# Chunk stages at fixed distances with feed-forward units spread evenly between them, in an RWKV-6 attention kernel with a leaky-ReLU feed-forward

## The chip, the cores and the metric

The kernel runs on one core of a Trainium2 chip. The metric is the device time of one execution in microseconds, the median of several runs. Beside the timed runs there is one profiled execution, whose span (from its first to its last instruction) and own time are given below.

A core has five engines that run side by side, each through its own instructions in a fixed order: PE (TensorE, matmuls and transposes; its weight loads are listed as PEld), DVE (VectorE), ACT (ScalarE), POOL (GpSimd) and SP (SyncE), which here only issues transfers. Matmul results land in PSUM, which has 8 banks of 128 x 512 f32.

## The reference

Attention with a decaying state: 4 batches, 8 heads, 768 steps, head size 48. The result goes through a feed-forward part with a leaky ReLU: 3072 tokens of 384 features, 2048 hidden features, 384 outputs.

```python
for t in range(S):
    cur = np.einsum('bhd,bhe->bhde', u[None] * kt, vt)
    y[:, :, t] = np.einsum('bhd,bhde->bhe', rt, state + cur)
    state = wt[:, :, :, None] * state + np.einsum('bhd,bhe->bhde', kt, vt)
x = y.transpose(0, 2, 1, 3).reshape(B * S, H * D)
h = x @ w_in
out = np.maximum(0.01 * h, h) @ w_out
```

## The kernel before

The tokens are cut into 24 chunks of 128, six to each batch. Within a chunk the recurrence is written as matrix products; between the chunks of a batch a state of 48 x 48 per head is carried on. A chunk goes through five stages, each a function that issues instructions on several engines:

- `s_decay` (lines 124 to 165) issues the chunk's four loads on SP, takes the logarithm of w (ACT, L131), sums it over the steps by two matmuls and four small ones into `cum` (PE, L133 to L140), takes the exponential (ACT, L141), and makes `rd`, `kd` and `el`, the decayed r and k and the decay of the whole chunk (DVE, L144, L145, L148). GpSimd makes `vb` (L151), the products r*u and r*u*k (`t1`, `t2`, L154, L156) and, after a sum on DVE (L160), `vsc` (L162), the part of a step that comes from its own k and v.
- `s_trans` (L167) transposes `rd` and `kd` on PE into `trp` (L172), and DVE copies it to `rkT` (L176).
- `s_scores` (L179) multiplies them into two banks `at` (L186), and DVE masks these into `mt` (L192).
- `s_mix` (L197) makes `y` on PE from the carried state (L206) and the scores (L212); DVE adds `vsc` and gives `ysb` (L218). Then it makes `kv` (L225), DVE adds the old state (`tt`, L232), and GpSimd multiplies by `el` into the next state `st` in two steps (L237). The next chunk's L206 needs that state.
- `s_out` (L244) transposes `ysb` on PE into `ytr` (L248), and ACT copies it into `xT` (L249), which holds all tokens, features across partitions.

The feed-forward part works on blocks of 256 tokens, two chunks. One unit of `m_hidden` (L257) fills a PSUM bank `hp` with two groups of 128 hidden features by 6 matmuls of 256 columns (L264), and ACT writes the leaky ReLU of it to `gt` (L268). One unit of `m_out` (L270) does 8 matmuls of 384 columns (L276) into `op`, half the sum over the hidden features for 128 tokens; after the second half ACT copies it to `osb` (L282) and SP sends it out (L284). A block is 8 hidden units and 4 output units.

PSUM: `cum` has two banks, `trp` and `ytr` share one, the tag `att` (`at` twice, `y`, `kv`) has three, and the tag `mlp` (`hp` and `op`) has two.

PE's order is the order in which the functions are called, under `manual_schedule`. The order on the other engines is made by the framework. The calls come from a small planner (L295 to L337) with costs and latencies of its own: a stage that is due goes first, and feed-forward units otherwise, as soon as their block's tokens are there; at most three chunks are under way. In the order that comes out, the twelve units of a block always stand together, and between two blocks stand some ten stages of two to four chunks. From the third block on, with a stage written by its first letter (D decay, T transposes, S scores, M mix, O out) and h and o for the units:

```
h2*8 o2*4 T7 M6 T8 S7 O6 D9 S8 M7 M8 T9 O7 D10 O8 D11 h3*8 o3*4 S9 T10 T11 S10 M9 S11 M10 O9 D12 M11 h4*8 o4*4
```

It begins with `D0 T0 S0 D1 M0 T1 O0 S1 D2 M1 T2 O1 h0*8 o0*4` and ends with `h10*8 o10*4 O22 O23 h11*8 o11*4`.

Of the kernel before, what the change touches and what calls it, by code (L numbers as in the profile page):

```python
# [8 lines left out]
F32 = mybir.dt.float32  # L9
BF16 = mybir.dt.bfloat16  # L10
AF = mybir.ActivationFunctionType
# [5 lines left out]
def kernel(  # L17
# [11 lines left out]
    nc = tc.nc  # L29
    B, H, S, D = r.shape  # L30
    L = 128
    assert S % L == 0 and H == 8 and D == 48
    C = S // L
    NCH = B * C
    NP = H // 2
    DM = H * D
    KT = DM // 128
    FF = moe_w_in.shape[1]
    NFT = FF // 128
    NOUT = moe_w_out.shape[1]  # L40
    MB = 256
    NBLK = B * S // MB
    CPB = MB // L
    assert DM % 128 == 0 and FF % 256 == 0 and (B * S) % MB == 0 and NOUT <= 512

    const = ctx.enter_context(tc.tile_pool(name="const", bufs=1))
    inpool = ctx.enter_context(tc.tile_pool(name="inpool", bufs=6))
    work = ctx.enter_context(tc.tile_pool(name="work", bufs=3))
    gpool = ctx.enter_context(tc.tile_pool(name="gpool", bufs=2))
    ps_cum = ctx.enter_context(tc.tile_pool(name="ps_cum", bufs=1, space=bass.MemoryType.PSUM))  # L50
    ps_tr = ctx.enter_context(tc.tile_pool(name="ps_tr", bufs=1, space=bass.MemoryType.PSUM))
    ps_att = ctx.enter_context(tc.tile_pool(name="ps_att", bufs=3, space=bass.MemoryType.PSUM))
    ps_mlp = ctx.enter_context(tc.tile_pool(name="ps_mlp", bufs=2, space=bass.MemoryType.PSUM))
# [5 lines left out]
        out=tri[:], in_=tri[:], compare_op=ALU.is_gt, fill=0.0, base=0,  # L59
# [5 lines left out]
        out=trin[:], in_=trin[:], compare_op=ALU.is_ge, fill=0.0, base=0,  # L65
# [20 lines left out]
    w_in_b = const.tile([128, KT, FF], BF16, name="w_in_b")  # L86
    w_out_b = const.tile([128, NFT, NOUT], BF16, name="w_out_b")
    xT = const.tile([128, KT, B * S], BF16, name="xT")
# [20 lines left out]
    for q in range(4):  # L109
        nc.gpsimd.dma_start(  # L110
            out=w_in_b[:, :, q * FQ : (q + 1) * FQ],
            in_=moe_w_in[:, q * FQ : (q + 1) * FQ].rearrange("(t p) n -> p t n", p=128),
        )
    for q in range(2):
        hf = NFT // 2
        nc.gpsimd.dma_start(
            out=w_out_b[:, q * hf : (q + 1) * hf, :],
            in_=moe_w_out[q * hf * 128 : (q + 1) * hf * 128, :].rearrange("(t p) n -> p t n", p=128),
# [3 lines left out]
    att = {}  # L122
# [120 lines left out]

    def s_out(i):  # L244
        a = att.pop(i)
        ytr = ps_tr.tile([128, KT, 128], BF16, name="ytr", tag="tr")
        for t in range(KT):
            nc.tensor.transpose(ytr[:, t, :], a["ysb"][:, t * 128 : (t + 1) * 128], ident[:])  # L248
        nc.scalar.copy(out=xT[:, :, i * L : (i + 1) * L], in_=ytr[:])  # L249

    stages = (s_decay, s_trans, s_scores, s_mix, s_out)


    gts = {}
    ops = {}

    def m_hidden(q, j2):  # L257
        if j2 == 0:
            gts[q] = gpool.tile([128, NFT, MB], BF16, name="gt")
        hp = ps_mlp.tile([128, 2, MB], F32, name="hp", tag="mlp")  # L260
        for jj in range(2):
            j = 2 * j2 + jj
            for t in range(KT):
                nc.tensor.matmul(  # L264
                    hp[:, jj, :], lhsT=w_in_b[:, t, j * 128 : (j + 1) * 128],
                    rhs=xT[:, t, q * MB : (q + 1) * MB], start=(t == 0), stop=(t == KT - 1),
                )
        nc.scalar.activation(out=gts[q][:, 2 * j2 : 2 * j2 + 2, :], in_=hp[:], func=AF.Prelu, alpha=0.01)  # L268

    def m_out(q, ts, hf):  # L270
        if hf == 0:
            ops[q, ts] = ps_mlp.tile([128, NOUT], F32, name="op", tag="mlp")
        op = ops[q, ts]
        half = NFT // 2
        for j in range(hf * half, (hf + 1) * half):
            nc.tensor.matmul(  # L276
                op[:], lhsT=gts[q][:, j, ts * 128 : (ts + 1) * 128], rhs=w_out_b[:, j, :],
                start=(j == 0), stop=(j == NFT - 1),
            )
        if hf == 1:  # L280
            osb = work.tile([128, NOUT], F32, name="osb")
            nc.scalar.copy(out=osb[:], in_=op[:])  # L282
            row = q * MB + ts * 128
            nc.sync.dma_start(out=out[row : row + 128, :], in_=osb[:])  # L284

    mlp = []
    for q in range(NBLK):
        for j2 in range(NFT // 2):
            mlp.append((q, 0.66, m_hidden, (q, j2)))
        for ts in range(CPB):  # L290
            for hf in range(2):
                mlp.append((q, 1.3, m_out, (q, ts, hf)))


    cost = (0.55, 0.6, 0.6, 1.0, 0.25)  # L295
    lat = (2.6, 1.2, 1.9, 1.2, 0.9)
    ready = {}
    for i in range(NCH):
        ready[i, 0] = 6.0 + 6.0 * i
    done_out = {}  # L300
    now = 0.0
    nxt = [0] * NCH
    head = 0
    m = 0
    AHEAD = 3
    with tc.manual_schedule(engines={mybir.EngineType.PE}):
        while head < NCH or m < len(mlp):
            cands = []
            for i in range(head, min(head + AHEAD, NCH)):
                s = nxt[i]  # L310
                if s < 5 and (s, i) and (i == 0 or nxt[i - 1] > s):
                    cands.append((ready[i, s], -s, i))
            cands.sort()
            mready = None
            if m < len(mlp):
                last = CPB * (mlp[m][0] + 1) - 1
                if last in done_out:
                    mready = done_out[last]
            if cands and (cands[0][0] <= now or mready is None or mready > now):
                t, s, i = cands[0]  # L320
                if mready is not None and mready < t:
                    now = max(now, mready)
                else:
                    s = -s
                    now = max(now, t) + cost[s]
                    stages[s](i)
                    nxt[i] = s + 1
                    ready[i, s + 1] = now + lat[s]
                    if s == 4:
                        done_out[i] = now + lat[4]  # L330
                        while head < NCH and nxt[head] == 5:
                            head += 1
                    continue
            q, t, f, args = mlp[m]
            now = max(now, mready) + t
            f(*args)
            m += 1  # L337


# [28 lines left out]
```

## Time and profile before

| | |
|---|---|
| Median of 3 runs | 312.15 us (311.21 to 316.01) |
| The profiled execution's own time | 311.16 us |
| Its span | 309.3 us |
| Mean granted TensorE clock | 0.865 of full speed |
| PE busy | 218.6 us, 1912 matmuls |
| PEld busy | 155.1 us, 1912 weight loads |
| ACT, DVE, POOL busy | 109.7, 106.0 and 104.4 us |
| Moved by DMA | 27.25 MB, mean 88 GB/s |

Times are in microseconds. A row of the costliest groups gives line, engine, operation, output<-input, shapes and count, then busy time and the mean of one in nanoseconds, then the idle time of the engine before them and what ended it. A row of the timeline gives start, duration, engine, line, operation and, in brackets, the idle time before it and its cause. Rows of the same kind that follow each other are merged, with a count. Matmul ends are modelled, so distances from start to start are the better measure of PE's pace.

### The profile page before, as it was taken

The page shows a single profiled execution, that of the slowest core. Times are in us where ns is not written, and L with a number is a line of the kernel's source. Part 1 is how long each engine was busy: PE and PEld are TensorE (multiplying, and loading weights), DVE is VectorE, ACT ScalarE, POOL GpSimd, SP SyncE. Part 2 cuts the span into 40 slices and gives each one's busy share as a digit, 9 for nine tenths or more (in the row PEclk, how much of TensorE's full clock was granted, in tenths as well). Part 3 has the DMA queues.
Part 4 walks back from the last instruction along what each step waited for, and adds up shares of the span by engine and source line. Part 5 has one row for each costly group of instructions (what it writes and reads, how often), then busy time and mean ns, then how long its engine had stood idle before and what let it go on. Part 6 is the DMA issues. An engine that isn't in the chain of part 4 may idle for free. (4 is left out here: it accounts for less than half of the span.)

```text
span 309.3 us, 4807 instructions
## 1 busy us (share of the span) xinstructions
PE 218.6 (71%) x1912; PEld 155.1 (50%) x1912; DVE 106.0 (34%) x220; ACT 109.7 (35%) x193; POOL 104.4 (34%) x152
## 2 busy tenths in 40 slices
PE   1005269736988946966979759858979489769895
PEld 0002147425756634744757447546656367457572
DVE  1015261447323284056020383094030750370000
ACT  2011135421737225502556127404474045204361
POOL 8012797175713165207203077055000250020000
PEclk9999999955899985995998958975999959956999
DMA  8999995799549265414336126120010000100001
GB/s 140 202 184 196 190 180 104 164 181 188 110 102 194 63 127 101 79 53 82 73 94 110 53 46 135 51 51 2 14 38 26 28 1 2 51 0 2 33 21 51
DMA packets 107143, 27.25 MB, mean 88 GB/s; under 512 B 100336, under 2 KB 107120, under 8 KB 107120
## 3 DMA queue, kind: packets, MB, share of 16 engines
q1 hardware_dynamic: 103440, 23.80, 40.9%
q0 software_dynamic: 3680, 3.15, 6.4%
q8 instruction: 15, 0.25, 0.4%
q14 instruction: 8, 0.07, 0.1%
HBM read 25.36 MB, written 4.72 MB: 97 GB/s over the span
## 5 line engine op out<-in xcount | busy, mean ns | idle before, releaser
L264 PE MATMUL hp<-xT,w_in_b 128*128 128x256 bf16 x576 | 83.5, 305 | 1.9 <-ACT xT L249 1.1
L264 PEld LDWEIGHTS <-w_in_b 128*128 128x128 bf16 x576 | 61.9, 109 | 21.3 <-issue 7.6
L268 ACT ACTIVATE gt<-hp 128x512 bf16<-128x512 f32 x96 | 57.3, 597 | 29.8 <-PE hp L264 27.3
L276 PE MATMUL op<-w_out_b,gt 128*128 128x384 bf16 x384 | 64.3, 326 | 0.2
L276 PEld LDWEIGHTS <-gt 128*128 128x128 bf16 x384 | 37.5, 98 | 24.9 <-issue 1.2
L151 POOL CAST vb<-v_in 128x384 bf16<-128x384 f32 x24 | 12.1, 504 | 99.1 <-PE kv L225 67.8
L192 DVE TENSOR_TENSOR mt<-at,tri 128x512 bf16<-128x512 f32 x48 | 30.9, 682 | 42.2 <-PE at L186 42.0
L249 ACT COPY xT<-ytr 128x384 bf16<-128x384 bf16 x24 | 11.6, 482 | 75.1 <-PE ytr L248 75.1
L154 POOL TENSOR_TENSOR t<-r_in,ukb 128x384 f32<-128x384 f32 x24 | 23.9, 997 | 39.7 <-DMA r_in<-in_r_dram 38.5
L144 DVE TENSOR_TENSOR rd<-cum,r_in 128x384 bf16<-128x384 f32 x24 | 13.3, 553 | 49.9 <-ACT cum L141 49.6
L176 DVE COPY rkT<-trp 128x1024 bf16<-128x1024 bf16 x24 | 16.4, 685 | 39.0 <-PE trp L172 39.0
L172 PE MATMUL trp<-ident,rd 128*128 128x128 bf16 x96 | 10.9, 245 | 26.7 <-DVE rd L144 17.1
L282 ACT COPY osb<-op 128x384 f32<-128x384 f32 x24 | 11.5, 479 | 50.9 <-PE op L276 50.9
L237 POOL TENSOR_TENSOR st<-tt,el 48x192 bf16<-48x192 f32 x40 | 20.1, 502 | 22.7 <-DVE tt L232 21.2
L156 POOL TENSOR_TENSOR t<-t,k_in 128x384 f32<-128x384 f32 x24 | 23.9, 996 | 9.2 <-DMA k_in<-in_k_dram 7.1
L141 ACT ACTIVATE cum<-cum 128x772 f32<-128x772 f32 x24 | 19.2, 802 | 15.0 <-PE cum L136 13.9
L206 PE MATMUL y<-st,rkT 128*128 128x96 bf16 x80 | 8.9, 255 | 20.5 <-POOL st L237 19.5
L172 PEld LDWEIGHTS <-rd 128*128 128x128 bf16 x96 | 7.4, 108 | 28.8 <-DVE rd L144 18.2
L131 ACT ACTIVATE lw<-w_in 128x384 bf16<-128x384 f32 x24 | 12.5, 520 | 24.6 <-DMA w_in<-in_w_dram 24.6
L160 DVE TENSOR_REDUCE diag<-t 128x8 f32<-128x384 f32 x24 | 13.2, 550 | 22.3 <-POOL t L156 15.7
L162 POOL TENSOR_TENSOR vsc<-v_in,diag 128x384 f32<-128x384 f32 x24 | 19.9, 830 | 2.3 <-DVE ysb L218 2.0
L248 PE MATMUL ytr<-ident,ysb 128*128 128x128 bf16 x72 | 10.2, 266 | 14.3 <-DVE ysb L218 7.7
(39 smaller groups left out, 178.3 us busy)
## 6 DMA issues: line engine op xcount, KB each, us to landing
w_in<-in_w_dram SPq DMA_DIRECT2D x24, 192.0 KB, 4.2
r_in<-in_r_dram SPq DMA_DIRECT2D x24, 192.0 KB, 3.7
k_in<-in_k_dram SPq DMA_DIRECT2D x24, 192.0 KB, 4.1
v_in<-in_v_dram SPq DMA_DIRECT2D x24, 192.0 KB, 3.6
out_dram<-osb SPq DMA_DIRECT2D x24, 192.0 KB, 1.9
w_in_b<-in_moe_w_in_dram POOLq DMA_DIRECT2D x4, 384.0 KB, 9.8
w_out_b<-in_moe_w_out_dram POOLq DMA_DIRECT2D x2, 768.0 KB, 19.2
ukb<-in_u_dram SPq DMA_DIRECT2D x1, 192.0 KB, 11.6
```

Of the source, the lines that this page charges most:

```text
L141: nc.scalar.activation(out=cum[:, 128:900], in_=cum[:, 128:900], func=AF.Exp)
L144: nc.vector.tensor_tensor(out=rd[:, :, 0:D], in0=e1, in1=a["r"][:], op=ALU.mult)
L154: nc.gpsimd.tensor_tensor(out=t1[:], in0=a["r"][:].rearrange("p h d -> p (h d)"), in1=ukb[:], op=ALU.mult)
L156: nc.gpsimd.tensor_tensor(out=t2[:], in0=t1[:].rearrange("p (h d) -> p h d", h=H), in1=a["k"][:], op=ALU.mult)
L162: nc.gpsimd.tensor_tensor(out=vsc[:], in0=a["v"][:], in1=diag[:].unsqueeze(2).to_broadcast([128, H, D]), op=ALU.mult)
L172: nc.tensor.transpose(trp[:, x, p, :], src[:, 2 * p : 2 * p + 2, :].rearrange("p h d -> p (h d)"), ident[:])
L176: nc.vector.tensor_copy(out=rkT[:], in_=trp[:])
L192: nc.vector.tensor_tensor(out=mt[:, x], in0=ats[x][:], in1=tri[:].unsqueeze(1).to_broadcast([128, NP, 128]), op=ALU.mult)
L237: nc.gpsimd.tensor_tensor(out=sn[r0 : r0 + D, :, x * D : (x + 1) * D], in0=tt[r0 : r0 + D, :, x * D : (x + 1) * D], in1=a["el"][r0 : r0 + ...
L264: nc.tensor.matmul(hp[:, jj, :], lhsT=w_in_b[:, t, j * 128 : (j + 1) * 128], rhs=xT[:, t, q * MB : (q + 1) * MB], start=(t == 0), stop=(t ...
L268: nc.scalar.activation(out=gts[q][:, 2 * j2 : 2 * j2 + 2, :], in_=hp[:], func=AF.Prelu, alpha=0.01)
L276: nc.tensor.matmul(op[:], lhsT=gts[q][:, j, ts * 128 : (ts + 1) * 128], rhs=w_out_b[:, j, :], start=(j == 0), stop=(j == NFT - 1),)
```

## The change

The planner is replaced by a fixed table. Stage s of chunk i stands at position 5i + 3s (the first three chunks apart: chunks 0 and 1 one after the other, chunk 2 at 10 + 2s). Units of a block are spread evenly, by their planned cost, from 1.5 positions behind the `s_out` of the block's last chunk to the same point of the next block; the last block has 20 positions. The calls are sorted by position.

The blocks are two of 256 tokens and then five of 512. A hidden unit of a 512-token block fills its bank with one group of 128 hidden features, by 3 matmuls of 512 columns; such a block has 16 hidden and 8 output units. `ytr` moves from the bank of `trp` to the three of `att`, and the pools of the inputs have eight buffers instead of six.

The order begins with `D0 T0 S0 M0 O0 D1 T1 S1 M1 O1 D2 h0*2 T2 h0*2 S2 D3 h0 M2 h0*2 O2 T3`, a steady part reads

```
T9 h2 M8 h2*2 D10 h2 S9 h2*2 O8 h2*2 T10 h2 M9 h2*2 D11 h2 S10 h2*2 O9 h2*2 T11 o2 M10 o2 D12 S11 o2 O10 o2 T12 o2
```

and it ends with `T23 o5 M22 o5 S23 o5 O22 o5*2 M23 o5*2 O23 o5 h6*16 o6*8`.

```diff
-    inpool = ctx.enter_context(tc.tile_pool(name="inpool", bufs=6))
+    inpool = ctx.enter_context(tc.tile_pool(name="inpool", bufs=8))
...
-        ytr = ps_tr.tile([128, KT, 128], BF16, name="ytr", tag="tr")
+        ytr = ps_att.tile([128, KT, 128], BF16, name="ytr", tag="att")
...
+    sizes = [256, 256] + [512] * ((B * S - 512) // 512)
+    starts = [sum(sizes[:n]) for n in range(len(sizes))]
...
+    def m_hidden(q, j, nj):
+        mb, t0 = sizes[q], starts[q]
+        if j == 0:
+            gts[q] = gpool.tile([128, NFT, mb], BF16, name="gt", tag="gt")
+        hp = ps_mlp.tile([128, nj, mb], F32, name="hp", tag="mlp")
+        for jj in range(nj):
             for t in range(KT):
                 nc.tensor.matmul(
+                    hp[:, jj, :], lhsT=w_in_b[:, t, (j + jj) * 128 : (j + jj + 1) * 128],
+                    rhs=xT[:, t, t0 : t0 + mb], start=(t == 0), stop=(t == KT - 1),
+                )
+        nc.scalar.activation(out=gts[q][:, j : j + nj, :], in_=hp[:], func=AF.Prelu, alpha=0.01)
...
+    def block_units(q):
+        units = []
+        nj = 512 // sizes[q]
+        for j in range(0, NFT, nj):
+            units.append((0.66, m_hidden, (q, j, nj)))
+        for ts in range(sizes[q] // 128):
             for hf in range(2):
+                units.append((1.3, m_out, (q, ts, hf)))
+        return units
...
+    def when(i, s):
+        if i < 2:
+            return 5 * i + s
+        if i == 2:
+            return 10 + 2 * s
+        return 5 * i + 3 * s
+    events = []
     for i in range(NCH):
+        for s in range(5):
+            events.append((when(i, s), 0, i, stages[s], (i,)))
+    avail = [when((starts[q] + sizes[q]) // L - 1, 4) + 1.5 for q in range(len(sizes))]
+    avail.append(avail[-1] + 20)
+    for q in range(len(sizes)):
+        units = block_units(q)
+        total = sum(t for t, _, _ in units)
+        done = 0.0
+        for n, (t, f, args) in enumerate(units):
+            pos = avail[q] + (avail[q + 1] - avail[q]) * done / total
+            events.append((pos, 1, n, f, args))
+            done += t
+    events.sort(key=lambda e: e[:3])
     with tc.manual_schedule(engines={mybir.EngineType.PE}):
+        for _, _, _, f, args in events:
             f(*args)
```

More of the change, by code (lines that the diff above doesn't have):

```diff
@@ L40 @@
     NOUT = moe_w_out.shape[1]
[L41 to L44, printed above, removed]
+    assert DM % 128 == 0 and FF % 256 == 0 and (B * S) % 512 == 0 and NOUT <= 512
     const = ctx.enter_context(tc.tile_pool(name="const", bufs=1))
-    inpool = ctx.enter_context(tc.tile_pool(name="inpool", bufs=6))
+    inpool = ctx.enter_context(tc.tile_pool(name="inpool", bufs=8))
     work = ctx.enter_context(tc.tile_pool(name="work", bufs=3))
@@ L251 @@
     stages = (s_decay, s_trans, s_scores, s_mix, s_out)
+    sizes = [256, 256] + [512] * ((B * S - 512) // 512)
+    assert sum(sizes) == B * S
+    starts = [sum(sizes[:n]) for n in range(len(sizes))]
     gts = {}
     ops = {}
[L257 to L262, printed above, removed]
+    def m_hidden(q, j, nj):
[4 more added lines that the diff above has]
+        for jj in range(nj):
             for t in range(KT):
                 nc.tensor.matmul(
-                    hp[:, jj, :], lhsT=w_in_b[:, t, j * 128 : (j + 1) * 128],
-                    rhs=xT[:, t, q * MB : (q + 1) * MB], start=(t == 0), stop=(t == KT - 1),
+                    hp[:, jj, :], lhsT=w_in_b[:, t, (j + jj) * 128 : (j + jj + 1) * 128],
+                    rhs=xT[:, t, t0 : t0 + mb], start=(t == 0), stop=(t == KT - 1),
                 )
-        nc.scalar.activation(out=gts[q][:, 2 * j2 : 2 * j2 + 2, :], in_=hp[:], func=AF.Prelu, alpha=0.01)
+        nc.scalar.activation(out=gts[q][:, j : j + nj, :], in_=hp[:], func=AF.Prelu, alpha=0.01)
     def m_out(q, ts, hf):
@@ L282, in m_out @@
             nc.scalar.copy(out=osb[:], in_=op[:])
-            row = q * MB + ts * 128
+            row = starts[q] + ts * 128
             nc.sync.dma_start(out=out[row : row + 128, :], in_=osb[:])
[L286 to L290, printed above, removed]
-            for hf in range(2):
-                mlp.append((q, 1.3, m_out, (q, ts, hf)))
-    cost = (0.55, 0.6, 0.6, 1.0, 0.25)
-    lat = (2.6, 1.2, 1.9, 1.2, 0.9)
@@ L297 @@
-    ready = {}
-    for i in range(NCH):
[L299 to L305, printed above, removed]
-    with tc.manual_schedule(engines={mybir.EngineType.PE}):
[L307 to L335, printed above, removed]
@@ L336 @@
             f(*args)
-            m += 1
 _INS = ['r', 'k', 'v', 'w', 'u', 'moe_w_in', 'moe_w_out']
```

## The prediction

> **What bounds the kernel now.** First the page's totals and its row of granted clock.
>
> ```profile
> span 309.3 us, 4807 instructions
> ...
> PE 218.6 (71%) x1912; PEld 155.1 (50%) x1912; DVE 106.0 (34%) x220; ACT 109.7 (35%) x193; POOL 104.4 (34%) x152
> ...
> PEclk9999999955899985995998958975999959956999
> ```
>
> TensorE is the busiest engine, but 90.7 us of the span (309.3 - 218.6) it does nothing, and in places it is granted only half of its clock. VectorE, ScalarE and GpSimd each work a third of the time: per chunk 106.0/24 = 4.4, 109.7/24 = 4.6 and 104.4/24 = 4.35 us. Nothing is full on average, so I looked at single stretches: all from the first feed-forward unit to just before the last block; one burst of attention stages; the eight hidden units of one block behind a burst with ScalarE still busy; the same after another burst; and the last block's hidden units.
>
> ```profile
> 44.30:293.60 249.30, 197.20 (x1740) 140.76 (x1740) 92.91 (x184) 96.41 (x171) 82.75 (x117) 0.84 0.37 74
> 57.36:77.61 20.25, 10.50 (x135) 8.21 (x135) 13.20 (x26) 5.50 (x10) 11.94 (x17) 0.62 1.19 192
> 94.48:100.50 6.02, 5.86 (x52) 4.67 (x49) 2.28 (x5) 5.08 (x9) 2.99 (x3) 1.00 1.12 191
> 253.17:260.70 7.53, 7.44 (x53) 5.53 (x51) 1.09 (x3) 4.98 (x8) 1.48 (x3) 0.76 0.00 1
> 294.20:300.20 6.00, 5.88 (x49) 4.65 (x49) 0.00 (x0) 4.18 (x7) 0.00 (x0) 1.00 0.01 4
> ```
>
> Columns: stretch, its length, busy PE, PEld, DVE, ACT, POOL, granted clock, DMA share, GB/s. A block runs dense; a burst leaves PE half idle at clock 0.62, with nothing from a block in it. What PE waits for from 57 us on:
>
> ```profile
> PE y L206 <- POOL st L237: 19.5, 12, 3.7
> PE trp L172 <- DVE rkT L176: 8.3, 7, 2.1
> PE cum L133 <- DVE el L148: 8.2, 5, 2.1
> ```
>
> These are waits between neighbours of one kind: the mix of chunk i+1 right behind that of i, needing its state; two transposes on one bank; two decays on one bank. So the middle is bound by chains of latency inside the bursts, not by any engine's work.
>
> **What the work costs when nothing waits.** From the chain of waits, two groups of 12 hidden matmuls and the last output units:
>
> ```profile
> 257.70 1.47 PE hp L264 x12
> ...
> 259.20 1.47 PE hp L264 x12
> ...
> 300.20 5.37 PE op L276 x32
> ```
>
> Twelve matmuls are two units and take 1.50 us, start to start: 0.75 us a unit. An output unit is 8 of 32: 1.34 us. The weight loads show that the hidden unit is not PE's own pace:
>
> ```profile
> 295.70 1.29 PEld L264 LDWEIGHTS <-w_in_b 128*128 128x128 bf16 x12 [0.20 <-issue]
> ```
>
> 1.30 us of work and 0.20 us of waiting: two hp banks go round, and the third unit waits until ScalarE (0.6 us, below) has emptied the first. Without that wait a unit is 0.65 us.
>
> ```profile
> L264 PE MATMUL hp<-xT,w_in_b 128*128 128x256 bf16 x576 | 83.5, 305 | 1.9 <-ACT xT L249 1.1
> ...
> L268 ACT ACTIVATE gt<-hp 128x512 bf16<-128x512 f32 x96 | 57.3, 597 | 29.8 <-PE hp L264 27.3
> ```
>
> Attention, from stretches at full clock, start to start:
>
> ```profile
> 57.29 0.40 PE L186 MATMUL at<-rkT 48*128 48x128 bf16 x8
> 57.62 0.34 PE L133 MATMUL cum<-lw,tri 128*128 128x384 bf16 x1
> ...
> 60.26 0.34 PE L133 MATMUL cum<-lw,tri 128*128 128x384 bf16 x1 [2.06 <-DVE el L148]
> ...
> 60.70 0.33 PE L206 MATMUL y<-st,rkT 128*128 128x96 bf16 x4
> ...
> 61.24 0.39 PE L172 MATMUL trp<-ident,rd 128*128 128x128 bf16 x4
> 61.46 0.39 PE L172 MATMUL trp<-ident,kd 128*128 128x128 bf16 x4
> ```
>
> ```profile
> 265.90 0.33 PE L248 MATMUL ytr<-ident,ysb 128*128 128x128 bf16 x3
> ...
> 266.07 0.33 PE L133 MATMUL cum<-lw,tri 128*128 128x384 bf16 x1
> ```
>
> Scores 57.62 - 57.29 = 0.33; decay 60.70 - 60.26 = 0.44; mix 61.24 - 60.70 = 0.54; transposes twice 0.22 = 0.44; s_out 0.17. Together 1.92 us a chunk.
>
> Now the profiled execution adds up: 44.3 to the first hidden unit; 96 x 0.75 + 48 x 1.34 = 136.3 of feed-forward; 22 chunks (0 and 1 are mostly done) x 1.92 = 42.2; 3.7 from the end of the last matmul (300.20 + 5.37) to 309.3. That is 226.5, so 82.8 us are lost to idling and low clock between. The execution was 311.16 us, 1.9 outside the span; the median is 1.0 more.
>
> **The change, part by part.**
>
> *Start.* PE now has decay 1 behind s_out 0, where it ran while chunk 0 was still under way. I take the other engines' early order as it is.
>
> ```profile
> 21.05 0.80 ACT L141 ACTIVATE cum<-cum 128x772 f32<-128x772 f32 x1
> 25.89 0.80 ACT L141 ACTIVATE cum<-cum 128x772 f32<-128x772 f32 x1 [4.04 <-PE cum L136]
> ```
>
> ```profile
> 24.89 0.50 PE L133 MATMUL cum<-lw,tri 128*128 128x384 bf16 x1
> ...
> 26.41 0.46 PE L212 MATMUL y<-vb,mt 128*128 128x48 bf16 x7 [0.38 <-DVE mt L192]
> ...
> 36.87 0.50 PE L248 MATMUL ytr<-ident,ysb 128*128 128x128 bf16 x3 [7.71 <-DVE ysb L218]
> ...
> 43.27 0.48 PE L248 MATMUL ytr<-ident,ysb 128*128 128x128 bf16 x3 [0.89 <-DVE rkT L176]
> 44.32 1.01 PE L264 MATMUL hp<-xT,w_in_b 128*128 128x256 bf16 x4 [0.57 <-ACT xT L249]
> ```
>
> Chunk 0's s_out ends at 37.4. Then chunk 1 alone: decay to exp 1.0 (24.89 to 25.89); exp to the end of its y 5.8 (21.05 to 26.87); ysb about 0.7; s_out to the first hidden unit 1.05 (43.27 to 44.32). First hidden unit at 46.0 instead of 44.3. If chunk 0's vsc were earlier, PE could be there by 36, which I keep as lower end.
>
> *512-column matmuls.* 240 of 512 columns and 96 of 256 stream the same columns as 576 of 256, fill the same 96 banks and need the same 96 ScalarE passes. The 240 weight loads saved lay beside other matmuls (12 in 1.30 us, the matmuls' own pace), so they save nothing. What saves is a stage between units: 80 units at 0.65; the 16 of the last block stand together and stay at 0.75. Hidden 64.0, output 64.3, in all 128.3. Ends: all 96 at 0.65 (126.7) and all at 0.75 (136.3).
>
> *Spreading, early.* From position 10.5 to 48.5 are 38 positions, or 7.6 chunks, with the two 256-token blocks: 21.1 us of feed-forward (2 x (8 x 0.65 + 4 x 1.34)) and 14.6 of attention, 4.7 us a chunk. There VectorE (4.4), GpSimd (4.35) and the loads (0.786 MB at 192 GB/s, 4.1) are nearly as long, in order, so I don't expect 4.7. The burst above moved three chunks in 20.25 us, 6.75 a chunk, with nothing between; that is the upper end. I take 6.0: a loss of 7.6 x 1.3 = 10.
>
> *Spreading, steady.* 16 chunk positions carry four 512-token blocks: half of them 8 hidden units (5.2 + 1.92 = 7.1 us), half 4 output units (5.4 + 1.92 = 7.3). The neighbours of one kind are now five positions apart, a stage and its successor three, 4.3 us; the waits of 1 to 2 us listed above go, under units of 0.65 to 1.34 us. If that cover were gone they would cost what they cost now. What is late next is ScalarE: 8 x 0.6 and (109.7 - 57.3 - 24 x 0.5)/24 = 1.7 of its own, 6.5 of 7.1 us. The row of 94.48 lets eight units through in 6.0 with 5.1 of ScalarE in them, so I put 0.4 a chunk, 6 in all; ends 0 and 1.6 a chunk (as in the row of 253.17, 7.53 for 6.0).
>
> *y transposes on the score banks.* This takes ytr out of trp's bank; five tiles a chunk now share three banks. The tiles in them are emptied a stage ahead, under at least one unit, so nothing; bare it would be one ysb, 0.56 us a chunk, 13 in all. *Eight input buffers:* no load is among PE's waits, so nothing. *The clock* I take as full where units stand between the stages.
>
> *Tail.* The last block is 512 tokens and starts after s_out 23: it is within the 128.3, but uncovered. I add 3 for ramps.
>
> Sum: 46.0 + 128.3 + 42.2 + (10 + 6 + 3) + 3.7 + 1.9 = 241.1 on the profiled execution's scale, **242 us** on the median's. With the ends of start, banks and losses: 36 + 126.7 + 42.2 + 3 + 5.6 = 214 to 46 + 136.3 + 42.2 + (16 + 26 + 3) + 13 + 5.6 = 288, not all at once: 228 to 262.
>
> **The rivals.** *ScalarE becomes the bound in hidden stretches.* Its order puts a pass behind an exp that waits for PE, and PE waits for the bank: 2.4 us more in each of 8 chunks and some in the early blocks, 25 in all: 267. For it, 91% load; against it, the row of 94.48.
>
> *The clock stays low.* The middle has 0.84 now. If the interleaved stretch kept that, 170.5 us of PE work would be 203, 32 more: 274. For it, the row of 253.17, where 0.76 made 6.0 into 7.5; against it, the rows at 1.00, where the bank's 0.20 us waits did no harm. The Trainium skill, TensorE: Matmul & The Clock Gate, in the section on PSUM-queue depth-cycling, speaks against this change: 512-column matmuls that idle briefly at each bank let the clock swing between half and full. The last row, waits and full clock together, does not bear it out.
>
> *Slower: the attention pace holds, and the longer tail is paid.* SP issues loads and output transfers in one order, and GpSimd's t and st stand in one order.
>
> ```profile
> SPq L284 <- ACT osb L282: 149.6, 20, 23.2
> ```
>
> ```profile
> POOL t L154 <- DMA r_in<-in_r_dram: 38.5, 12, 12.6
> ```
>
> ```profile
> L154 POOL TENSOR_TENSOR t<-r_in,ukb 128x384 f32<-128x384 f32 x24 | 23.9, 997 | 39.7 <-DMA r_in<-in_r_dram 38.5
> ...
> L237 POOL TENSOR_TENSOR st<-tt,el 48x192 bf16<-48x192 f32 x40 | 20.1, 502 | 22.7 <-DVE tt L232 21.2
> ...
> r_in<-in_r_dram SPq DMA_DIRECT2D x24, 192.0 KB, 3.7
> ```
>
> A load queued behind an output lands 3.7 us after it, then two t of 1.0 and two st of 0.5: 6.7 us until the state is there and the next mix can run, of which two output units cover 2.7. 4.0 a chunk makes the period 11.2, what it is now (249.3/22 = 11.3): 46 + 22 x 11.2 + 12 + 10.7 + 5.6 = 321. It decides from 3.8 us a chunk. Against it: the waits of GpSimd fell under blocks, and loads run chunks ahead.
>
> *Wide matmuls cost less than their columns.* If 512 columns took no longer than 384 do now, 5.37/32 = 168 ns instead of 650/3 = 217, 240 of them would save 12 us: 230. Against it, both widths that the trace shows go by their columns, 108 ns for 256 and 168 for 384. The Trainium skill, same page, section on the back-to-back issue gap, gives about 131 ns for 512 columns among weight loads; as an estimate from that page the sum would be 221, which the 168 ns for 384 columns contradict.
>
> **How the numbers follow.** Forecast 0.58; ScalarE 0.14; clock 0.12; slower 0.07; the wide matmuls or the early start, below 228, together 0.04; in between, the loss half gone to new waits and the time unchanged, 0.05. Range 226 to 284: the forecast, ScalarE's case and most of the clock's, about 0.82. The measurement tells 2%, 6 us, from no change: faster 0.88, same 0.05, slower 0.07.
>
> **What would show it.** Right: first hp near 46 us; PE's waits for st, rkT and el together under 10 us; granted clock 0.95 or more behind 60 us; ScalarE's idle time behind hp small until the last block; 336 loads of w_in_b; about 23 us of pure feed-forward at the end; about 6 us a chunk to 93, then near 7.5. Wrong: hp waiting for gt in each hidden stretch (ScalarE), fives in the clock row (clock), y waiting for st behind t and an input (slower), or a first hp past 50.

## The result and the profile after

The changed kernel takes 231.61 us (231.19 to 232.03, four runs) against 312.06 us: a ratio of 0.7435, 95% interval 0.7411 to 0.746. The ratio is of the fast runs alone; one run of the kernel before, of 316.01 us, was a slow one. The forecast was 242, its range 226 to 284. The profiled execution took 231.19 us with a span of 229.5.

The changed kernel's page: the lines that answer to those shown before, with PE's busy tenths in 40 slices and the group of ScalarE's leaky ReLU:

```profile
span 229.5 us, 4321 instructions
...
PE 180.8 (79%) x1659; PEld 111.8 (49%) x1672; DVE 106.5 (46%) x220; ACT 106.2 (46%) x193; POOL 103.8 (45%) x152
...
PE   1000402379889998999999999999999999999993
...
PEclk9999999999999999999999999999999999999999
...
L268 ACT ACTIVATE gt<-hp 128x512 bf16<-128x512 f32 x96 | 57.4, 598 | 17.9 <-PE hp L264 15.6
```

The other engines do what they did. PE is idle 48.7 us (229.5 - 180.8) instead of 90.7, and its work counts 180.8 us instead of 218.6: of the 79.8 us that the span lost, 42 were idle time and 38 were matmuls that took longer, at low clock or with a wait for a bank inside a run. (The matmuls' ends are modelled, so this split is rough.) The granted clock is full in every slice of its row. For the first 51 us the row says little, there as in the kernel before: the transposes of chunk 1 take 0.61 us and stand 0.46 apart, those of chunk 2 take 0.39 and stand about half as far apart (timeline of PE):

```profile
43.31 0.61 PE L169 MATMUL trp<-ident,rd 128*128 128x128 bf16 x4 [4.27 <-DVE rd L141]
...
51.83 0.39 PE L169 MATMUL trp<-ident,rd 128*128 128x128 bf16 x4
```

What PE waits for in the whole execution:

```profile
PE trp L169 <- DVE rd L141: 25.0, 6, 18.9
PE ytr L245 <- DVE ysb L215: 9.1, 2, 8.8
PE cum L130 <- ACT lw L128: 4.6, 1, 4.6
PE y L209 <- DVE mt L189: 2.4, 4, 0.9
PE at L183 <- DVE rkT L173: 1.9, 3, 0.8
PE at L183 <- DVE ysb L215: 0.4, 1, 0.4
PE hp L264 <- ACT xT L246: 0.3, 1, 0.3
```

The waits of the middle for `st` (19.5 us), `rkT` (8.3, by `trp`) and `el` (8.2) are gone. The 1.9 us for `rkT` are waits of another stage, the scores, and two of the three lie in chunks 0 and 1, as all the long waits do. Stretches of the changed kernel (length, PE, PEld, DVE, ACT, POOL, clock, DMA share, GB/s): the two short blocks, one steady round of four chunks and a block, and the last block but for its first 0.4 us:

```profile
49.84:90.31 40.47, 37.31 (x434) 27.40 (x432) 30.63 (x64) 22.81 (x42) 29.27 (x40) 1.00 0.80 145
...
133.78:162.45 28.67, 28.51 (x270) 17.49 (x272) 17.68 (x34) 17.30 (x33) 11.56 (x18) 1.00 0.30 58
...
203.49:225.58 22.09, 22.07 (x110) 10.56 (x109) 0.00 (x0) 11.27 (x20) 0.00 (x0) 1.00 0.10 36
```

In the steady round PE is busy 28.51 of 28.67 us, and 28.67 is its work: 16 hidden units at 0.65, 8 output units at 1.30 and four chunks at 1.92 make 28.5. From 90 us on the kernel is bound by PE's own pace, but for the 16 hidden units of the last block: these stand together and take 11.95 us instead of 10.3.

### The profile page after: what moved, and what is told of

Read it like the earlier page. It is cut to its first block, busy times and chain, and to the rows that moved or that the text cites. A ratio compares the mean times of both kernels' runs of the same rounds, so it can differ in the third digit from the quotient of the medians.

```text
span 229.5 us, 4321 instructions
## 1 busy us (share of the span) xinstructions
PE 180.8 (79%) x1659; PEld 111.8 (49%) x1672; DVE 106.5 (46%) x220; ACT 106.2 (46%) x193; POOL 103.8 (45%) x152
## 4 chain that ended last, share of the span: by engine, by line
PE 62%; POOL 13%; DMA 9%; issue 8%; DVE 4%; SPq 1%; ACT 1%; POOLq 0%; DVEq 0%; ACTq 0%
PE op L276 25%; PE hp L264 23%; DMA ukb<-in_u_dram 6%; POOL t L153 4%; POOL t L151 3%; PE trp L169 3%; PE at L183 2%; POOL vsc L159 2%; PE y L209 2%; DMA r_in<-in_r_dram 2%; DMA w_in<-in_w_dram 2%; POOL st L234 2%; POOL vb L148 2%; DVE mt L189 1%; SPq L96 1%
## 5 line engine op out<-in xcount | busy, mean ns | idle before, releaser
L264 PE MATMUL hp<-xT,w_in_b 128*128 128x512 bf16 (+1 forms) x323 | 72.6, 350 | 1.0 <-ACT xT L246 0.3
L276 PE MATMUL op<-w_out_b,gt 128*128 128x384 bf16 x384 | 68.9, 326 | 0.0
L268 ACT ACTIVATE gt<-hp 128x512 bf16<-128x512 f32 x96 | 57.4, 598 | 17.9 <-PE hp L264 15.6
L276 PEld LDWEIGHTS <-gt 128*128 128x128 bf16 x384 | 35.4, 98 | 21.3 <-issue 0.2
L264 PEld LDWEIGHTS <-w_in_b 128*128 128x128 bf16 x336 | 30.2, 98 | 23.1 <-issue 3.7
L189 DVE TENSOR_TENSOR mt<-at,tri 128x512 bf16<-128x512 f32 x48 | 31.7, 683 | 4.8 <-PE at L183 4.4
L169 PE MATMUL trp<-ident,rd 128*128 128x128 bf16 x96 | 9.8, 227 | 25.0 <-DVE rd L141 25.0
L169 PEld LDWEIGHTS <-rd 128*128 128x128 bf16 x96 | 6.9, 100 | 29.1 <-DVE rd L141 26.7
L215 DVE TENSOR_TENSOR ysb<-y,vsc 128x384 bf16<-128x384 f32 x24 | 13.4, 556 | 15.2 <-PE y L209 13.9
L245 PE MATMUL ytr<-ident,ysb 128*128 128x128 bf16 x72 | 8.3, 226 | 9.1 <-DVE ysb L215 9.1
```

The costliest lines, as they stand in the source:

```text
L169: nc.tensor.transpose(trp[:, x, p, :], src[:, 2 * p : 2 * p + 2, :].rearrange("p h d -> p (h d)"), ident[:])
L189: nc.vector.tensor_tensor(out=mt[:, x], in0=ats[x][:], in1=tri[:].unsqueeze(1).to_broadcast([128, NP, 128]), op=ALU.mult)
L264: nc.tensor.matmul(hp[:, jj, :], lhsT=w_in_b[:, t, (j + jj) * 128 : (j + jj + 1) * 128], rhs=xT[:, t, t0 : t0 + mb], start=(t == 0), stop= ...
L268: nc.scalar.activation(out=gts[q][:, j : j + nj, :], in_=hp[:], func=AF.Prelu, alpha=0.01)
L276: nc.tensor.matmul(op[:], lhsT=gts[q][:, j, ts * 128 : (ts + 1) * 128], rhs=w_out_b[:, j, :], start=(j == 0), stop=(j == NFT - 1),)
```

## The experiments

My theory had two parts: the units between the stages cover the stages' latencies (A), and with that the clock stays up (A2). The rivals: the wide matmuls and blocks bring the gain (B); the new order of stages alone brings it, as no two of one kind stand side by side any more (C). Each ratio is to the kernel before on the same chip; the changed kernel's is 0.7435.

**The units of a block together again.**

```diff
-            pos = avail[q] + (avail[q + 1] - avail[q]) * done / total
+            pos = avail[q]
```

> All else as in the changed kernel, but the units of a block stand together at its first position, so that the attention stages of two or four chunks stand side by side, at their table distances, with nothing between them. Theory A (the units between the stages cover their latencies): the chains come back. Per chunk about 2 us from decay to transposes, 1.1 from scores to mix and some for the state, 3.5 us on 22 chunks: about 305 us, with the granted clock back under 0.9. Rival C (the order of the stages does it: no neighbours of one kind any more): short waits only, 240 to 250 us. Rival B (the 512-column blocks do it): 232 us.

Measured: 294.83 us, 0.9455 (0.9398 to 0.9512). Of the 80 us gained, 63 go with this one line, though the order of the stages among themselves is the new one. Rivals B and C fall; A stands, its size somewhat too large. The page's clock row, parts of one burst (timeline of PE), and that burst in two halves (columns as before):

```profile
PEclk9999999995598699999589997599995799986999
```

```profile
127.68 0.33 PE L203 MATMUL y<-st,rkT 128*128 128x96 bf16 x4
...
135.23 0.40 PE L169 MATMUL trp<-ident,rd 128*128 128x128 bf16 x4 [0.80 <-DVE rd L141]
...
136.88 0.33 PE L203 MATMUL y<-st,rkT 128*128 128x96 bf16 x4 [0.78 <-POOL st L234]
...
144.50 0.61 PE L169 MATMUL trp<-ident,rd 128*128 128x128 bf16 x4 [0.56 <-DVE rd L141]
145.36 0.63 PE L264 MATMUL hp<-xT,w_in_b 128*128 128x512 bf16 x1
```

```profile
127.68:136.88 9.20, 5.61 (x85) 3.94 (x83) 8.07 (x16) 3.67 (x7) 6.50 (x10) 1.00 0.53 107
136.88:145.36 8.48, 7.07 (x78) 5.03 (x78) 6.81 (x15) 3.19 (x6) 6.56 (x10) 0.52 1.00 185
```

Four chunks' stages take 17.7 us here (127.68 to 145.36), 4.4 a chunk instead of 1.92. The single waits are short, at most 1.2 us, but the clock goes too: the same transposes take 0.40 us at 135 and 0.61 at 144. The low clock doesn't make this burst longer: its second half, at 0.52, takes no more time than the first at full clock. What the low clock costs shows behind the bursts, where the next hidden units begin slowly.

So the 63 us are made up as follows (timeline of PE). The six bursts take 95.8 us for some 42 of work, 54 more. The hidden units take 79.3 us instead of 63.6, 16 more: 8 of these because 80 of them stand together again at 0.75, the rest mostly low clock. Less the 7.4 us that the changed kernel itself loses (worked out in the section on the prediction), this makes 62; the spans differ by 61.5. One thing stays open: the order on the other engines changes with the table too, and no run holds it fixed.

**All blocks of 256 tokens.**

```diff
-    sizes = [256, 256] + [512] * ((B * S - 512) // 512)
+    sizes = [256] * (B * S // 256)
...
-    avail.append(avail[-1] + 20)
+    avail.append(avail[-1] + 10)
```

> The changed kernel with all blocks of 256 tokens (576 hidden matmuls of 256 columns again), spread in the same way. Theory A: width costs nothing, 231 to 233 us; the last block is shorter, but PE's work is the same. Rival B (wide matmuls and 240 fewer weight loads carry the gain): 250 us or more.

Measured: 229.28 us, 0.7355 (0.7325 to 0.7386), a little less than with the wide blocks. The 240 weight loads and the width are worth nothing; the wide blocks even cost some 2 us. 0.8 of these is what eight more dense hidden units in the last block cost at 0.1 each, 0.6 an earlier first hidden unit (49.2 us); the rest I can't name.

**Blocks of 512 under the planner.**

```diff
-    MB = 256
+    MB = 512
...
-        hp = ps_mlp.tile([128, 2, MB], F32, name="hp", tag="mlp")
+        hp = ps_mlp.tile([128, MB], F32, name="hp", tag="mlp")
```

The rest of the hidden unit follows: one group of 128 features in place of two, 16 units a block.

> The kernel before, planner and all, with blocks of 512 tokens. Theory A: the bursts stay, fewer and longer, 300 to 316 us. Rival B: most of the gain, 250 us or less.

Measured: 305.84 us, 0.9816 (0.9769 to 0.9864): 6 us from half as many bursts, as A has it.

**The stages of a chunk nearer to each other.**

```diff
-        return 5 * i + 3 * s
+        return 5 * i + s
```

> The changed kernel with the stages of a chunk one position apart instead of three (5i + s), still with a unit behind nearly every stage. Theory A (cover must be as long as the latency): one position is about 1.4 us; decay to transposes needs 2.4 us behind PE's last decay matmul and gets 1.0, scores to mix 1.7 and gets 1.1, so about 2 us a chunk on 21 chunks: 270 to 280 us. Rival (any unit between two stages is enough, it is the mixing that counts): 232 to 238 us.

> The changed kernel with the stages two positions apart (5i + 2s). Theory A: decay to transposes now gets 2.9 - 0.4 = 2.4 us of cover for 2.4 us of latency and scores to mix 2.4 for 1.7: 0 to 0.5 us a chunk lost, 231 to 242 us, far nearer to distance 3 (231.6) than to distance 1 (272). Rival (the loss grows in proportion as the distance falls): 251 us.

The second has `5 * i + 2 * s`. Measured: 272.26 us at distance 1 (0.8729, 0.8651 to 0.8807), 236.21 at 2 (0.7576, 0.7526 to 0.7626), 231.6 at 3. 36 us are lost from 2 to 1, 5 from 3 to 2: a threshold near the latency, not a proportion. At distance 2 every wait of PE of 0.2 us or more lies before 94 us. At distance 1, one chunk from its decay to its mix (timeline), and the two largest groups of PE's waits, which include the start:

```profile
152.69 0.24 PE L133 MATMUL cum<-ones,lw 128*128 128x1 bf16 x4
152.79 1.46 PE L276 MATMUL op<-w_out_b,gt 128*128 128x384 bf16 x8
153.06 0.81 ACT L138 ACTIVATE cum<-cum 128x772 f32<-128x772 f32 x1
...
153.90 0.56 DVE L141 TENSOR_TENSOR rd<-cum,r_in 128x384 bf16<-128x384 f32 x1 [2.21 <-ACT cum L138]
...
154.51 0.40 PE L169 MATMUL trp<-ident,rd 128*128 128x128 bf16 x4 [0.26 <-DVE rd L141]
...
156.61 0.40 PE L183 MATMUL at<-rkT 48*128 48x128 bf16 x8
...
156.94 0.34 PE L203 MATMUL y<-st,rkT 128*128 128x96 bf16 x4
...
157.79 0.20 PE L209 MATMUL y<-vb,mt 128*128 128x48 bf16 x1 [0.51 <-DVE mt L189]
...
158.38 0.35 PE L209 MATMUL y<-vb,mt 128*128 128x48 bf16 x7 [0.40 <-DVE mt L189]
```

```profile
PE trp L169 <- DVE rd L141: 33.2, 22, 17.7
PE y L209 <- DVE mt L189: 17.5, 37, 0.8
```

```profile
PEclk9999999999999999999999999999999999999999
```

One output unit covers 1.3 of the 1.7 us from the start of that unit to the transposes. Between scores and mix of this chunk no unit stands at all, and `mt` is waited for twice. By the waits this is the larger loss: `mt` has 17.5 us instead of the changed kernel's 2.4, `rd` 33.2 instead of 25.0. Theory A expected it the other way about, 1.4 us a chunk for `rd` and 0.6 for `mt`; decay to transposes needs 1.8 us (152.69 to 154.51) and not 2.4. So the total of 2 us a chunk came out by two errors that offset each other. The clock stays full all the same, although PE is idle 28 us more than in the changed kernel (270.2 - 193.3 = 76.9 against 48.7): waits of up to 1.1 us between units didn't pull it down, the bursts without units did.

**The bursts of the kernel before filled with matmuls that nobody reads.**

```diff
                     stages[s](i)
+                    if 1 <= s <= 3:
+                        keep = ps_mlp.tile([128, 2, MB], F32, name="keep", tag="mlp")
+                        for n in range(4):
+                            nc.tensor.matmul(
+                                keep[:, n % 2, :], lhsT=ident[:], rhs=xT_keep[:], start=True, stop=True,
+                            )
```

> The kernel before with four matmuls of 256 columns on a constant tile, written to a feed-forward bank and read by nobody, behind each of the stages transposes, scores and mix: 72 x 0.43 = 31 us of added PE work at full clock. Theory A2 (of the 83 us lost about 31 go to the low clock, the rest to waits in which the filling fits): clock back over 0.95, the units behind a burst at 0.75 us from the first one, about 300 us in spite of the added work. Rival (the clock costs little, all is waiting): 312 to 335 us, as the filling stands in the chains.

Measured: 308.07 us, 0.9879 (0.984 to 0.9918), mean clock 0.961 instead of 0.865. Faster with 31 us of work added, but by 4 us and not by 12. Most blocks behind a burst now run as if there had been none (timeline):

```profile
253.75 5.97 PE L267 MATMUL hp<-xT,w_in_b 128*128 128x256 bf16 x48 [0.16 <-ACT xT L252]
259.75 5.36 PE L279 MATMUL op<-w_out_b,gt 128*128 128x384 bf16 x32
```

6.0 us for the eight units that took 7.5 before. All twelve such groups together take 74.7 us instead of 83.7, where 0.75 a unit would be 72. So A2 is right in its direction: the clock had a price, 9 us of it in the hidden units. What more of the 83 us it was, inside the bursts, can't be read from this run, since the filling lies partly in waits and partly in the chains. The first hidden unit comes later, too, at 47.9 us instead of 44.3.

**The small edits.** Both undone, then each alone (`ytr` back with `ps_tr`, `inpool` back to six):

> The changed kernel with ytr back in the bank of trp and six input buffers. Theory A: both are covered, 231 to 233 us. Rival: PE's waits of ytr for rkT and of trp for xT come back, 5 us or more, 237 us and up.

> The changed kernel with ytr back in the bank of trp, but eight input buffers. If the 4.7 us that the two small edits were worth together are the bank's (PE's wait of trp for xT, 3.8 us, where s_out and the next transposes stand side by side), 235 to 236.5 us again; if they are the two buffers', 231.5 to 232.5 us.

> The changed kernel with six input buffers instead of eight, ytr on the score banks as changed. If the 4.5 us between the run with both small edits undone (236.3) and the one with only ytr undone (231.8) are the buffers', loads come late: 235.5 to 237 us, with SP waiting for the GpSimd and VectorE steps that free a buffer and a ScalarE or GpSimd step waiting for an input in the stretch from 85 to 200 us. If they need both edits, 231 to 233 us.

Measured: both 236.3 us (0.7581, 0.7547 to 0.7615), `ytr` alone 231.83 (0.7444, 0.7398 to 0.7491), six buffers alone 234.71 (0.7532, 0.7479 to 0.7584). The wait of `trp` for `xT` comes back with `ytr` alone too (3.8 us in six waits between 58 and 91 us) and yet the whole is no longer. About half of it stands where the changed kernel's transposes wait for `rd` (1.8 us in four waits between 63 and 80 us); where the rest is made up I did not find. The buffers are worth 3 us alone. The waits from 85 to 205 us have the first of these two lines with six buffers and the second with eight:

```profile
POOL t L151 <- DMA r_in<-in_r_dram: 18.8, 7, 3.8
```

```profile
POOL t L151 <- DMA r_in<-in_r_dram: 6.5, 6, 2.8
```

With six, SP's issues of loads (L96) now also wait for steps that read the inputs, for which they waited 0.5 us (`rd`) or not at all (`vsc`) with eight:

```profile
SPq L96 <- DVE rd L141: 9.4, 8, 4.3
SPq L96 <- POOL vsc L159: 8.8, 2, 5.8
```

And PE has one wait in the steady part that the changed kernel hasn't (timeline with six):

```profile
149.66 0.40 PE L169 MATMUL trp<-ident,rd 128*128 128x128 bf16 x4 [1.67 <-DVE rd L141]
```

GpSimd, in its order, waits for inputs that came late because the buffers came free late. What of that goes through which engine to PE's 1.67 us I did not follow; and the two edits undone together cost 1.6 us more than the buffers alone, which is within the intervals.

**The start.** Two edits of the first 50 us, and then both with short blocks.

```diff
         if i < 2:
-            return 5 * i + s
+            return ((0, 1, 2, 4, 6), (3, 5, 7, 8, 9))[i][s]
```

> The changed kernel with the first two chunks overlapped as in the kernel before (D0 T0 S0 D1 M0 T1 O0 S1 M1 O1). Theory A (PE-bound behind the first hidden unit): the first hidden unit comes at 44 to 46 us instead of 49.8 and the whole is as much shorter, 226 to 228 us. Rival (the loads or the other engines set the pace of the early chunks): the gain is lost again by 90 us, 231 us.

Measured: 225.58 us, 0.7216 (0.7161 to 0.7271). The first hidden unit comes at 43.8 us instead of 49.8, and the whole is 6.0 us shorter: in this run a microsecond at the first hidden unit is one at the end.

```diff
+    def load_w_in(vb):
+        for q in range(4):
+            nc.gpsimd.tensor_copy(out=w_in_b[:, 0, q * FQ : q * FQ + 1], in_=vb[:, 0:1])
+            nc.gpsimd.dma_start(
...
         for _, _, _, f, args in events:
             f(*args)
+            if f is s_decay and args[0] == 1:
+                load_w_in(att[1]["vb"])
+            if f is s_decay and args[0] == 2:
+                load_w_out(att[2]["vb"])
```

> The changed kernel with the feed-forward weights loaded behind chunk 1's v (w_in) and chunk 2's v (w_out) instead of beside the first chunks: a one-column copy on GpSimd ahead of each load makes it wait. Theory A (the start is bound by transfers, 3.1 MB of weights that nobody needs before the first hidden unit): the first hidden unit near 28 us, the whole 208 to 214 us. Rival (the loads of chunks and weights are needed by 50 us in any order): no gain, 230 us or a little more.

Measured: 220.03 us, 0.7038 (0.6983 to 0.7094). The first hidden unit is at 26.7 us, 23 earlier, but only half of that reaches the end. Between 27 and 45 us PE waits again (timeline):

```profile
32.58 0.52 ACT L114 ACTIVATE lw<-w_in 128x384 bf16<-128x384 f32 x1 [4.87 <-DMA w_in<-in_w_dram]
...
33.64 2.52 PE L269 MATMUL hp<-xT,w_in_b 128*128 128x256 bf16 x12 [3.38 <-ACT gt L273]
...
37.99 0.99 POOL L137 TENSOR_TENSOR t<-r_in,ukb 128x384 f32<-128x384 f32 x1 [9.28 <-DMA r_in<-in_r_dram]
...
39.96 0.55 DVE L143 TENSOR_REDUCE diag<-t 128x8 f32<-128x384 f32 x1 [8.97 <-POOL t L139]
...
42.88 1.28 DVE L175 TENSOR_TENSOR mt<-at,tri 128x512 bf16<-128x512 f32 x2
...
43.62 0.22 PE L195 MATMUL y<-vb,mt 128*128 128x48 bf16 x1 [5.26 <-DVE mt L175]
```

Twice an input of a later chunk is late. First `lw` of that chunk waits on ScalarE, ahead of the leaky ReLU that would empty a bank, and PE waits 3.38 us for the bank. Then `t` waits on GpSimd; `diag` of that chunk stands on VectorE ahead of `mt` of an earlier one and holds it; PE waits 5.26 us for `mt`. SP's issues of input loads take 4.3 to 5.6 us each from 18 to 38 us, and about 1.0 shortly before; in that time the weights are under way beside them. The clock, too, falls for a few microseconds there (0.976 in the mean). Both the theory (the start is bound by transfers) and its rival hold in part.

The last run has the weights later still (`w_out` in halves, behind the `v` of chunks 3 and 4), the overlapped start and blocks of 256:

> Three findings together: weights behind the first chunks (w_in behind chunk 1's v, the halves of w_out behind those of chunks 3 and 4), the first two chunks overlapped, blocks of 256 tokens. Theory A (PE-bound from the first hidden unit on): first hidden unit at 22 to 26 us, 2 us less for the short blocks, about 5 us of waits for chunk 4's loads in ScalarE's, VectorE's and GpSimd's order as in the run before: 206 to 214 us. Rival (transfers set the pace up to 50 us whatever the order): no better than 218 us.

Measured: 215.41 us, 0.6886 (0.6795 to 0.6977), first hidden unit at 25.2: the fastest here, 7% under the changed kernel, just above the expected stretch. The three gains don't add up: 2.3, 6.0 and 11.6 us off 231.6 would be 211.7. PE's waits name what is left:

```profile
PE trp L155 <- DVE rd L127: 6.4, 1, 6.4
PE hp L268 <- ACT gt L272: 5.6, 2, 4.1
...
PE op L280 <- DMA w_out_b<-in_moe_w_out_dram: 2.6, 1, 2.6
```

## Why the prediction was right, and where it was off

The sign, the mechanism and the range held; the forecast was 10 us too long. Two of its terms erred in opposite directions, the start by 3.8 us and the losses by 11.6, so that the sum is nearer than its largest term. Term by term, for the profiled execution:

| Term | Forecast | Measured |
|---|---|---|
| First hidden unit | 46.0 | 49.8 |
| Hidden units | 64.0 | 63.6 (80 x 0.645; 16 in 11.95) |
| Output units | 64.3 | 62.6 (48 x 1.30, and 0.16 of drain) |
| Attention, 22 chunks | 42.2 | 42.2, taken over |
| Lost between | 19 | 7.4, what remains |
| End and outside the span | 5.6 | 5.6 |
| Sum | 241.1 | 231.2 |

**Start: the step "I take the other engines' early order as it is" failed by 3.8 us.** Chunk 0's s_out started 0.9 us later than before, and VectorE had another order (timeline of the changed kernel, DVE):

```profile
42.23 0.55 DVE L157 TENSOR_REDUCE diag<-t 128x8 f32<-128x384 f32 x1 [1.80 <-POOL t L153]
42.70 0.55 DVE L141 TENSOR_TENSOR rd<-cum,r_in 128x384 bf16<-128x384 f32 x1
```

Chunk 1's `rd` could have started at 39.9, when its exp was done; a `diag` that waits for GpSimd stands ahead of it: 2.8 us.

**Output unit: mis-sized.** 5.37 us for 32 matmuls includes the drain of the last one; start to start it is 1.30 a unit, 1.7 us less in all.

**Losses: mis-sized, 7.4 instead of 19.** Early, a chunk took 40.47/7.6 = 5.3 us, not 6.0: the burst that I took for the upper end had its waits between neighbours, which the table had already taken apart. By the order, 33.9 us of work stand in these 40.47, so 6.6 were lost instead of 10. Steady, I charged 0.4 a chunk for ScalarE and 3 for ramps, 9 in all. About 1 of it came: from 90.31 to the last block at 203.05 PE takes 112.7 us for 111.5 of work, and a chunk takes 28.67/4 = 7.2 us, not the 7.5 that I gave as a sign. (The two losses are 0.4 more than the table's 7.4, because one decay counted in the 42.2 stands before the first hidden unit.) PE's list has no wait for `gt`; in the last block the bank's wait does come, inside a run of matmuls, at 0.75 a unit as forecast (ScalarE's timeline: two passes in 1.32, then 0.17 to 0.18 idle):

```profile
206.16 1.32 ACT L268 ACTIVATE gt<-hp 128x512 bf16<-128x512 f32 x2 [0.17 <-PE hp L264]
```

**Right by their own runs:** the width saves nothing (blocks of 256 are 2 us faster); the cover must be as long as the latency (the three distances); `ytr` on the score banks is worth nothing (231.8). **Wrong: "Eight input buffers: no load is among PE's waits, so nothing".** They are worth 3 us. With two buffers fewer the loads come late to GpSimd, and PE's one new wait is for VectorE; a list of PE's own waits doesn't name the loads.

**The rivals.** ScalarE: its idle time behind `hp` is 15.6 us and PE waits for no `gt`. Clock: 0.998. The swing that the Trainium skill describes (TensorE: Matmul & The Clock Gate, the section on PSUM-queue depth-cycling) is not seen in the changed kernel, nor at distance 1. Wide matmuls: 0.645/3 = 215 ns for 512 columns, by the columns. The 131 ns of the Trainium skill (same page, the section on the back-to-back issue gap) are not reached in any run here. Slower: no `t` holds `st` long enough to make `y` wait; PE has no wait for `st` in the list above.

## What to carry to other kernels

Where two kinds of work share one in-order engine, put units of the dense kind between the stages of the latency-bound kind, at a distance no shorter than the latency between two stages. Here the step from two positions to three brought 5 us and the step from two to one cost 36; more than three was not tried. The order did more than the sizes of the tiles: one line of the table carried 63 of 80 us. When the engine is then full to the end, a microsecond before its first dense unit can be worth one at the end, so look at what the first transfers carry. It was worth one when chunk 1 began earlier, and half of one when the weights moved, as these then held up later inputs.

## What the runs showed of the hardware that I had not expected

- The clock fell in stretches of a dozen microseconds or more with only attention stages (0.62 in the burst of the kernel before, 0.52 in the second half of one with the units together). It stayed full at distance 1, where waits up to 1.1 us stand between dense units, though these added 28 us of idle PE. That second burst had no wait over 1.2 us either, so the length of a single wait doesn't tell the two apart. How much dense work between the waits is enough was not measured.
- 512 columns go at 215 ns (six matmuls in 1.29 us), 384 at 163 ns (1.30/8) and 256 at 108 ns each in a run with weight loads: by the columns, with the loads hidden in all three.
- Moving 3.1 MB of weights behind the first chunks gave 23 us at the first hidden unit and 11.6 at the end: the transfers' pace came back as a wait of PE for ScalarE (3.38 us) and one for VectorE (5.26 us), the latter two engines away from the load that was late.
